# Joining the pair sums of the first two rounds on VectorE in 45 more attention jobs, and a later start for the last unit's W1 loads

## The chip, the core and the metric

The kernel is one program on one core of a Trainium2 chip. The metric is the device time of one execution in microseconds (us). The core has five engines with a queue each: TensorE (PE) multiplies matrices into the accumulator memory PSUM, ScalarE (ACT) evaluates functions, VectorE (DVE) adds, multiplies and copies, GpSimd (POOL) does small helper work, and SyncE (SP) starts all transfers. Each engine takes its instructions strictly in the order in which they were written, and waits at an instruction until the semaphores that it names have their values.

## The reference: a transformer layer

The input x has 2048 tokens of 1024 values, in bf16.

```python
h  = x + softmax((Q @ K.T) * 32**-0.5) @ V  joined over 32 heads of 32, @ wo    # Q, K, V = layernorm(x) @ wqkv
h2 = h + gelu_tanh(layernorm(h) @ w1 + b1) @ w2 + b2                             # w1: 1024 x 3584, w2: 3584 x 1024
```

Softmax needs, for each head and query, the sum of its 2048 exponentials. The kernel leaves out the maximum, keeps exp(scores) unnormalised in bf16, multiplies it with V, and divides by that sum at the end.

## The kernel before

**Jobs and rounds.** Queries are cut into 8 blocks of 256 (`qb` 0 to 7), heads into 8 groups of four (`g`). One pair (qb, g) is a job of 8 rounds; a round treats 256 keys. In a round PE computes the scores of four heads with 8 matmuls (`Att.qk`, line 838) into four PSUM banks; ACT turns them into probabilities with two exponentials of 128x1024 (line 850) written to a tile PT of a ring of nine. Then PE multiplies them with V (`Job.pv`, line 879). There are 512 rounds, or 1024 exponentials. The score step of a round needs PSUM banks that an earlier exponential has emptied. Groups 6 and 7 of the blocks 6 and 7 are done as two halves of 128 queries and 4 rounds each, so that the last unit can be finished half by half.

**The sums.** The denominators come from PE too: a matmul with a matrix of ones (`den`, line 918) adds up the probabilities over the keys of a tile. To spare PE, VectorE first adds the two 128-key halves of a round's tile PT into a tile PS (line 894, 128x1024 in bf16); `den` then takes 4 matmuls for a round instead of 8. The last round of a job is summed directly from PT. In whole jobs of the query blocks 6 and 7 (`four`, with the rounds in `FOURS`) the PS tiles of rounds 0 and 1, 2 and 3, 4 and 5 are also added to each other (line 901, the join), so that one `den` serves two rounds. PS is a ring of three tiles. When the job is over, five small VectorE instructions (lines 936 to 949) divide and write the attention output OT.

**The three lead jobs** (g = 0, qb = 0 to 2) run while the projections are still being computed; they sum every second round directly.

**Feed-forward work.** It is cut into 8 units of 256 tokens. For unit u, `wo` projects the attention output and adds x, `ln2` normalises, `ffn1` multiplies with W1 in 14 blocks of 512 KB (tile a_w1r, a ring of four), `evict1` (line 1049) adds the bias, `gelu` does five VectorE steps and a tanh on ACT (line 1067), and `ffn2` multiplies with W2 in two column halves j of 7 blocks each (tile a_w2r, a ring of seven). This work needs the attention of its own query block and fills PE between the rounds of later blocks. Unit 7 is done by halves of 128 tokens at the end: `wo(7)`, `ln2(7)`, `ffn1_half` and `ffn2_tile`; its W1 blocks are loaded once, to 14 places of their own (`W1B`, tile w1b), where K and V of the head groups 0 to 6 have been, and the second half of W2 goes to the tile w2b, where PT has been.

**The matmul helper.** `mm` writes a matmul either as one instruction (line 599 or 602) or as four of 32 columns (line 596) when it stands among other column-tiled ones.

**The order.** No engine's order is written out by hand. Every operation is a `Task` with engine, cost, priority and the tasks that it depends on, and `Graph.schedule` plays the program through once at build time with a table of costs and writes down the order that comes out. For PE it takes a ready score step first, then probabilities times V and sums, then feed-forward matmuls. On VectorE a lower number goes first: -2 for the sums and joins, 0 for evictions, 1 for gelu. On SP large loads of priority 1 may have three and of priority 2 two before them under way. A change of a dependency therefore moves instructions everywhere after it, on all engines, and the order is then fixed.

**Loads of the last unit's W1.** `load_w1_last` makes the 14 loads with priority 2; each waits for the last reader of the K or V that it overwrites. Between the profile's 899 and 1025 us they are issued among those of a_w1r, wov and a_w2r.

The tail of the program is this:

```python
    ffn1(6)
    load_w1_last()
    wo(7, (0,))
    ffn2(6, 0)
    ln2(7, (0,))
    ffn2(6, 1)
    ffn1_half(0, False)
    wo(7, (1,), True)
    ln2(7, (1,), True)
```

Of the kernel before, what the change touches and what calls it, by code (L numbers as in the profile page):

```python
# [12 lines left out]
P = 128  # L13
# [345 lines left out]
def build_kernel(nc, A_x, A_wqkv, A_wo, B_w1, B_b1, B_w2, B_b2, out):  # L359
# [7 lines left out]
    DC = D // P  # L367
# [9 lines left out]
    gr = Graph(N_LANES)  # L377
# [77 lines left out]
    for kind, k in (("x", 1), ("W", 4), ("x", 0), ("x", 2), ("x", 3), ("W", 3), ("W", 5), ("W", 0), ("W", 1)):  # L455
        h, b = sb(ph0, ("xnT%d" if kind == "x" else "Wall%d") % k, [P, DC, 512], BF, 1, 4)
# [19 lines left out]
    for k in range(2):  # L476
        h, b = sb(xq_lo, "xq%d" % k, [P, DC, 512], BF)
# [87 lines left out]
    def slot(nrel=1):  # L565
        return Slot(gr.buf(), nrel, (6, 7))
# [48 lines left out]
    def dma(out_ap, in_ap, nbytes, reads=(), writes=(), prio=0, noncontig=False, after=()):  # L615
        def fn(s):
            if noncontig:
                with nc.allow_non_contiguous_dma(reason="strided gather"):
                    return s.dma_start(out_ap, in_ap)
            return s.dma_start(out_ap, in_ap)  # L620
        return gr.add(E.SP, fn, 0.06, 0.0, reads, writes, prio, nbytes=nbytes, after=after)
# [234 lines left out]
    PV_START = 7  # L856

    closing = set()
    FOURS = (0, 2, 4)

    class Job:

# [8 lines left out]
        def pv(self, r, s):  # L871
            g, bank, first, nq = self.g, self.bank, self.n == 0, self.nq
            kt = 512 // nq
            last = self.n == self.nr - 1
            self.n += 1
            fns = []
            for i in range(kt):
                for h in range(4):
                    fns.append(lambda p, i=i, h=h: p.matmul(  # L879
                        psum[32 * h:32 * h + 32, bi(bank), 0:nq], V[:, g, kt * r + i, 32 * h:32 * h + 32],  # L880
                        PTs[s][:, h // 2, h % 2, nq * i:nq * i + nq], start=first and i == 0, stop=last and i == kt - 1,
                        tile_position=(0, 32 * h), skip_group_check=True))
            rd = B_PTs[s] + B_V[NT * g + kt * r:NT * g + kt * r + kt]
            t = pe(fns, 0.2222 if kt == 2 else 0.2255, reads=rd, writes=[self.B_O, self.B_D] if first else [self.B_O], kind="pv", mode="col")
            take(t, bank)
            while self.sums:
                self.den(*self.sums.pop(0), False)
            if last or self.g == 0 and self.qb < NLJ and r % 2:
                self.sums.append((s, True))
            else:  # L890
                n = cnt["ps"] % NS
                cnt["ps"] += 1
                pairs = PTs[s][:, :, :, :].rearrange("p u j c -> p (u j) c")
                dve(lambda v: v.tensor_tensor(PS[:, n, :, :], pairs[:, :, 0:256], pairs[:, :, 256:512], ALU.add), c_dve(1024, 2),  # L894
                    reads=B_PTs[s], writes=[B_PS[n]], prio=-2, after=hold if self.g == 0 and self.qb < NLJ else ())
                four = nq == 256 and self.qb >= 6
                if four and r in FOURS:
                    self.half = n
                elif four and r - 1 in FOURS:
                    o = self.half  # L900
                    dve(lambda v: v.tensor_tensor(PS[:, n, :, :], PS[:, n, :, :], PS[:, o, :, :], ALU.add), c_dve(1024, 2),
                        reads=[B_PS[n], B_PS[o]], writes=[B_PS[n]], prio=-2)
                    self.sums.append((n, False))
                else:
                    self.sums.append((n, False))
            if last:
                while self.sums:
                    self.den(*self.sums.pop(0), not self.sums)
                self.finish()
# [70 lines left out]
    def wblock(R, src_ap, prio=1, block=None):  # L980
        s = R.next("w1", R.nw1)
        if block is not None:
            dma(R.w1[:, s, :, :], w1d[block], P * DC * 512, reads=[B_w1d[block]], writes=[R.B_w1[s]], prio=prio)
            return s
        dma(R.w1[:, s, :, :], src_ap.rearrange("(dc p) c -> p dc c", p=P), P * DC * 512, writes=[R.B_w1[s]], prio=prio)
        return s
# [48 lines left out]
    def ffn1(u):  # L1035
        R = R1
        for blk in range(FC // 2):
            s = wblock(R, None, block=blk)
            bank = slot()
            for f in range(2):  # L1040
                for dc in range(DC):
                    mm(bank, R.w1[:, s, dc, f * P:(f + 1) * P], hnT[:, dc, :], dc == 0, dc == DC - 1,
                       [R.B_w1[s]] + B_hnT, True, (256 * f, 256 * f + 256))
            evict1(u, gT, B_gT, 2 * blk, 2, 256, bank)
            if blk % 2:
                gelu(gT, B_gT, 4 * (blk // 2), 4, 256)
# [22 lines left out]
        dve(lambda v: v.tensor_tensor(g, w, g, ALU.mult), c_dve(m, 2), reads=b + [B_uu[i]], writes=b, prio=1)  # L1069

    w1_last = []

    def load_w1_last():
        for k, (h, b) in enumerate(W1B):
            dma(h[:, :, :], w1d[k], P * DC * 512, reads=[B_w1d[k]], writes=[b], prio=2)
            w1_last.append((h, b))

    def ffn1_half(t, tail):
# [69 lines left out]
    NLJ = 3  # L1148
# [282 lines left out]
```

## Time and profile before

| what | value |
|---|---|
| runs | 1072.92, 1080.01, 1078.2 us; median 1078.2 |
| profiled execution | 1075.04 us, span of its instructions 1073.2 |
| granted TensorE clock | 1.00 |
| busy: PE, ACT, DVE, POOL | 1043.1, 1008.1, 783.6, 49.1 us |
| exponentials into PT (line 850) | 992, busy 924.6 us |
| pair sums PS from PT (line 894) | 427, busy 280.2 us, mean 685 ns |
| joins (line 901) | 36, median 691 ns |
| matmuls with ones (line 918) | 1692 from PS, busy 108.7 us |
| 512 KB loads, median to landing | a_w1r 4.2, a_w2r 4.6, w1b 3.9 us |

The profile is one execution. "Busy" is the time in which an engine had at least one instruction under way; on PE the ends of matmuls are modelled, so that a full PE is not a PE at its peak. Instructions that follow each other overlap at their ends, so the distance from start to start is shorter than the mean duration. The idle time of an engine that does not set the end costs nothing.

### The profile page before, as it was taken

What the parts mean: (1) busy time and instruction counts of PE and PEld (TensorE: products, weight loads), DVE (VectorE), ACT (ScalarE), POOL (GpSimd) and SP (SyncE); (2) the same over time, 40 slices, a digit from 0 to 9 for tenths busy, and PEclk for the clock granted to TensorE, in tenths of its full rate; (3) what the DMA queues carried; (4) which work ended last, traced back from release to release, by engine and by line L of the source; (5) the groups of instructions that cost most, each with busy time, mean ns of one, the idle gap of its engine ahead of it and who ended that gap; (6) DMA issues with size and microseconds to landing.
All of it is one profiled execution on the core that took longest, in us unless ns stands there. A gap on an engine that the chain in (4) does not pass through costs nothing.

```text
span 1073.2 us, 39708 instructions
## 1 busy us (share of the span) xinstructions
PE 1043.1 (97%) x17978; PEld 605.2 (56%) x17978; DVE 783.6 (73%) x1521; ACT 1008.1 (94%) x1117; POOL 49.1 (5%) x110
## 2 busy tenths in 40 slices
PE   8999999999999999999999999999999999998998
PEld 6576555554445744664475466447546644663575
DVE  8766666566677995797499569759978958987560
ACT  4999999999999999999999999999999999999732
POOL 4200000000000010001000000100010000000000
PEclk9999999999999999999999999999999999999999
DMA  8460544334665546846565684656377444876530
GB/s 236 110 184 23 175 135 120 120 119 153 207 207 160 193 160 187 281 148 217 185 222 173 179 271 166 220 177 227 125 237 253 173 153 148 271 265 227 202 131 16
DMA packets 130649, 192.04 MB, mean 179 GB/s; under 512 B 47024, under 2 KB 95024, under 8 KB 127920
## 3 DMA queue, kind: packets, MB, share of 16 engines
q1 hardware_dynamic: 130480, 189.50, 54.3%
q8 instruction: 141, 2.31, 0.8%
q14 instruction: 28, 0.23, 0.1%
HBM read 175.32 MB, written 26.21 MB: 188 GB/s over the span
## 4 chain that ended last, share of the span: by engine, by line
PE 61%; ACT 31%; DMA 3%; DVE 3%; issue 1%; POOL 0%; SPq 0%; DVEq 0%; POOLq 0%
PE ps L599 29%; ACT PT L850 28%; PE ps L838 10%; PE ps L596 7%; PE ps L879 7%; PE ps L918 4%; PE ps L602 3%; ACT PX L850 2%; DMA a_w2r<-w_blocks 2%; ACT uu L1067 2%; DMA a_w1r<-w_blocks 1%; DVE PS L894 1%; PE ps L1144 1%; PE ps L669 0%; DVE hch L1121 0%
## 5 line engine op out<-in xcount | busy, mean ns | idle before, releaser
L850 ACT ACTIVATE PT<-ps 128x1024 bf16<-128x1024 f32 x992 | 924.6, 1176 | 9.1 <-PE ps L838 8.6
L894 DVE TENSOR_TENSOR PS<-PT 128x1024 bf16<-128x1024 bf16 x427 | 280.2, 685 | 76.9 <-PE ps L918 39.0
L838 PE MATMUL ps<-QT,KT 32*128 32x256 bf16 (+1 forms) x4352 | 203.6, 266 | 9.3 <-ACT PT L850 6.6
L879 PE MATMUL ps<-PT,V 128*32 128x256 bf16 (+1 forms) x4224 | 160.6, 267 | 3.0 <-ACT PT L850 1.8
L838 PEld LDWEIGHTS ps<-QT,KT 32*128 32x128 bf16 x4352 | 64.4, 92 | 163.9 <-ACT PT L850 149.4
L599 PE MATMUL ps<-a_w2r,gT 128*128 128x512 bf16 x609 | 152.1, 381 | 4.5 <-DVE gT L1069 1.6
L599 PE MATMUL ps<-hnT,a_w1r 128*128 128x256 bf16 x1165 | 143.3, 273 | 2.7 <-DMA a_w1r<-w_blocks 2.2
L599 PEld LDWEIGHTS ps<-hnT,a_w1r 128*128 128x128 bf16 x1165 | 107.0, 98 | 33.6 <-issue 17.8
L879 PEld LDWEIGHTS ps<-PT,V 128*32 128x32 bf16 x4224 | 101.5, 97 | 25.7 <-issue 8.9
L918 PE MATMUL ps<-PS,ones 128*32 128x256 bf16 (+1 forms) x1692 | 108.7, 268 | 1.0 <-DVE PS L894 0.8
L599 PEld LDWEIGHTS ps<-a_w2r,gT 128*128 128x128 bf16 x609 | 52.0, 98 | 74.7 <-issue 19.7
L1049 DVE TENSOR_TENSOR gT<-ps,b1f 128x512 bf16<-128x512 f32 x98 | 67.4, 687 | 21.2 <-PE ps L596 13.1
L599 PE MATMUL ps<-xnT,Wall 128*128 128x512 bf16 (+1 forms) x364 | 79.9, 355 | 0.2 <-ACT xnT L676 0.2
L1067 ACT ACTIVATE uu<-uu 128x1024 bf16<-128x1024 bf16 (+1 forms) x53 | 61.6, 1182 | 14.2 <-DVE uu L1066 14.2
L1121 DVE SCALAR_TENSOR_TENSOR hch<-ps,hch 128x512 bf16<-128x512 f32 x32 | 21.9, 685 | 72.5 <-PE ps L599 39.3
L596 PE MATMUL ps<-hnT,a_w1r 128*32 128x256 bf16 x1612 | 61.0, 274 | 2.1 <-issue 1.7
L599 PE MATMUL ps<-wov,OT 128*128 128x512 bf16 x224 | 56.0, 380 | 0.0
L918 PEld LDWEIGHTS ps<-PS,ones 128*32 128x32 bf16 x1692 | 43.0, 96 | 18.9 <-DVE PS L894 6.7
L653 POOL CAST mvb<-mv 128x2 bf16<-128x2 f32 (+1 forms) x25 | 6.3, 253 | 983.0 <-DVE mv L650 983.0
L596 PE MATMUL ps<-a_w2r,gT 128*32 128x512 bf16 x700 | 50.2, 381 | 0.0
L599 PEld LDWEIGHTS ps<-xnT,Wall 128*128 128x128 bf16 x364 | 31.2, 98 | 32.8 <-issue 9.6
L596 PEld LDWEIGHTS ps<-hnT,a_w1r 128*32 128x32 bf16 x1612 | 40.8, 96 | 12.4 <-issue 10.7
(102 smaller groups left out, 995.6 us busy)
## 6 DMA issues: line engine op xcount, KB each, us to landing
a_w2r<-w_blocks SPq DMA_DIRECT2D x105, 512.0 KB, 4.6
a_w1r<-w_blocks SPq DMA_DIRECT2D x98, 512.0 KB, 4.2
wov<-wo_blocks SPq DMA_DIRECT2D x16, 1024.0 KB, 4.8
w_blocks<-in_B_w_dram SPq DMA_DIRECT2D x28, 512.0 KB, 3.9
w1b<-w_blocks SPq DMA_DIRECT2D x14, 512.0 KB, 3.9
Wall<-in_A_wqkv_dram SPq DMA_DIRECT2D x17, 256.0 KB, 4.5
xrb<-in_A_x_dram SPq DMA_DIRECT2D x16, 256.0 KB, 5.0
a_w1r<-in_A_wqkv_dram SPq DMA_DIRECT2D x8, 512.0 KB, 4.8
```

The source lines that it names most:

```text
L596: fns.append(lambda p, j=j: p.matmul(psum[32 * j:32 * j + 32, bi(bank), c0:c1], lhsT[:, 32 * j:32 * j + 32], rhs, start=start, stop=stop, ...
L599: t.whole = lambda p: p.matmul(psum[:, bi(bank), c0:c1], lhsT, rhs, start=start, stop=stop, skip_group_check=True)
L602: t = pe(lambda p: p.matmul(psum[:, bi(bank), c0:c1], lhsT, rhs, start=start, stop=stop), occ, reads=reads, writes=[bb(bank)], mode="full" ...
L838: return p.matmul(psum[:, 2 * us[h // 2] + h % 2, n * i:n * i + n], KT[32 * h:32 * h + 32, g, k0:k0 + P], QT[32 * h:32 * h + 32, qs, q0:q0 ...
L850: act(lambda a, u=u, k=k: a.activation(PTs[s][:, k, :, :], psum[:, 2 * u:2 * u + 2, :], ACT.Exp, bias=0.0, scale=SCALE), 1024, reads=[B_ps ...
L879: fns.append(lambda p, i=i, h=h: p.matmul(psum[32 * h:32 * h + 32, bi(bank), 0:nq], V[:, g, kt * r + i, 32 * h:32 * h + 32], PTs[s][:, h / ...
L894: dve(lambda v: v.tensor_tensor(PS[:, n, :, :], pairs[:, :, 0:256], pairs[:, :, 256:512], ALU.add), c_dve(1024, 2), reads=B_PTs[s], writes ...
L918: fns.append(lambda p, h=h, rhs=rhs, i=i: p.matmul(psum[32 * h:32 * h + 32, bi(bank), 256:256 + nq], ones32[:, :], rhs, start=False, stop= ...
L1049: t = dve(lambda v: v.tensor_tensor(g[:, fc:fc + nf, :], psum[:, bi(bank), :].rearrange("p (f c) -> p f c", f=nf), b1f[:, fc:fc + nf].unsq ...
L1067: act(lambda a: a.activation(w, w, ACT.Tanh, bias=0.0, scale=KT2), m, reads=[B_uu[i]], writes=[B_uu[i]], prio=-1)
L1121: drop(dve(lambda v: v.scalar_tensor_tensor(hch[:, hs, c], psum[:, bi(bank), :], half, hch[:, hs, c], ALU.mult, ALU.add), c_dve_ps(512), r ...
L1144: pe(lambda p: p.matmul(psum[:, 6, 0:256], ident[:, :], b2t[:, 0:256], start=True, stop=True), 0.18 if k < 42 else 0.115, reads=[B_ident, ...
```

## The change

There are two parts. In the first, the join of rounds 0 and 1 is done in all whole jobs but the three lead jobs; blocks 6 and 7 keep their three joins. In the second, `ffn1(6)` notes its 14 W1 loads, and all 14 loads of the last unit's W1 depend on the eleventh of them (`w1_loads[10:11]`).

```diff
@@ Job.pv
-    FOURS = (0, 2, 4)
...
-                four = nq == 256 and self.qb >= 6
+                four = nq == 256 and not (self.g == 0 and self.qb < NLJ)
+                FOURS = (0, 2, 4) if self.qb >= 6 else (0,)
                 if four and r in FOURS:
                     self.half = n
                 elif four and r - 1 in FOURS:
@@ ffn1
             s = wblock(R, None, block=blk)
+            if u == 6:
+                w1_loads.append(gr.tasks[-1])
@@ load_w1_last
+    w1_loads = []
...
-            dma(h[:, :, :], w1d[k], P * DC * 512, reads=[B_w1d[k]], writes=[b], prio=2)
+            dma(h[:, :, :], w1d[k], P * DC * 512, reads=[B_w1d[k]], writes=[b], prio=2, after=w1_loads[10:11])
```

The join itself is the same code as before:

```python
                    o = self.half
                    dve(lambda v: v.tensor_tensor(PS[:, n, :, :], PS[:, n, :, :], PS[:, o, :, :], ALU.add), c_dve(1024, 2),
                        reads=[B_PS[n], B_PS[o]], writes=[B_PS[n]], prio=-2)
                    self.sums.append((n, False))
```

## The prediction

> **What bounds the kernel now.** I read the totals first, then the 40 slices, then busy time by stage, then ScalarE's waits, the chain, and last the timeline of the end. TensorE (PE) and ScalarE (ACT) look equally full in the totals:
>
> ```profile
> PE 1043.1 (97%) x17978; PEld 605.2 (56%) x17978; DVE 783.6 (73%) x1521; ACT 1008.1 (94%) x1117; POOL 49.1 (5%) x110
> ...
> ACT  4999999999999999999999999999999999999732
> ```
>
> The slices show where ACT is not full: in the first and in the last three. The stages (us, then busy time and count of PE, PEld, VectorE (DVE), ACT, POOL, then clock, DMA share, GB/s) say it in numbers:
>
> ```profile
> 81.30:340.00 258.70, 256.34 (x4370) 135.32 (x4363) 168.07 (x311) 258.63 (x283) 3.99 (x8) 1.00 0.46 141
> 340.00:400.00 60.00, 60.00 (x1089) 38.10 (x1087) 55.24 (x107) 60.00 (x67) 1.53 (x4) 1.00 0.49 175
> ...
> 855.00:920.00 65.00, 59.23 (x1232) 29.43 (x1233) 48.23 (x103) 63.52 (x70) 3.76 (x8) 1.00 0.51 173
> 920.00:962.00 42.00, 39.77 (x767) 28.73 (x769) 37.24 (x68) 40.06 (x45) 0.00 (x0) 1.00 0.76 267
> 962.00:1013.10 51.10, 46.79 (x969) 22.84 (x961) 35.47 (x73) 50.78 (x56) 2.01 (x4) 1.00 0.61 209
> 1013.10:1073.20 60.10, 56.37 (x706) 39.80 (x698) 23.66 (x51) 15.36 (x37) 1.53 (x4) 1.00 0.27 97
> ```
>
> From 81 to 1013 us ACT works without a break: its idle time, stage by stage, sums to 5.8 us of 932. What it does there is fixed: exponentials (one per 0.92 us back to back: 47.79 us for 52 in the chain) and the 49 tanh of units 0 to 6. After 1013.1 it is almost done, and PE carries the last 60.1 us (56.4 busy). So the end is the last exponential plus a PE tail, and time can only come from ACT's 5.8 us or from the tail. ACT's waits in that stretch:
>
> ```profile
> ACT PT L850 <- PE ps L838: 5.6, 9, 1.4
> ACT PT L850 <- PE ps L879: 0.3, 1, 0.3
> ```
>
> Always a late score matmul. The larger ones are 1.08 us at 423 (PE waited 1.40 for W2), 1.25 at 881 (PE's 1.16 before it is put down to issue), 1.36 at 944 and 0.57 at 961. The last two belong to the second last unit's W1, which the chain shows as loads:
>
> ```profile
> 930.99 5.84 DMA a_w1r<-w_blocks
> ...
> 937.28 5.20 DMA a_w1r<-w_blocks
> ...
> 952.65 4.88 DMA a_w1r<-w_blocks
> ```
>
> These take 4.9 to 5.8 us where the kernel's median for such a load is 4.2, with 267 GB/s moved, since w1b loads for the last unit run between them.
>
> **The joins: what goes, what comes.** Query blocks 0 to 5 have 48 jobs; three lead jobs are left out, so 45 get one join. Each drops one denominator step of 4 column-tiled matmuls, 0.11 us on PE (929.50 in the chain): 45 x 0.11 = **5.0 us of PE**. Each adds one 128x1024 add on VectorE. The rows give it two prices: 0.69 alone (the 36 joins of blocks 6 and 7: median 691 ns) and 2.51 us for four in a row at 739.89, a step of (2.51 - 0.69)/3 = 0.61. Busy engines queue, so I take 0.61: 45 x 0.61 = **27 us of VectorE**, 3% of the 932 us.
>
> The 5.0 us are worth what ACT waits less, not 5.0 us. In the changed program's order the feed-forward work does run ahead: ffn2 of unit 6 ends in score round 506 instead of 512 (a round is one score step and two exponentials, 1.84 us). But wo of unit 7 needs the first half's attention output and begins in round 509, where it began in 507. PE will stand idle instead. Gain between 0 and the 1.6 us of ACT's idle time that neither a load nor issue explains (5.8 less 1.08, 1.25, 1.36 and 0.57 is 1.6); I take **0**, since nothing shows that these fragments come from lack of PE time.
>
> The 27 us of VectorE hide while VectorE has room. At 81 to 340 it is 65% busy. At 340 to 400, a ffn1 stretch, it is 92% busy, and its order is fixed: evictions, gelu steps and sums queue behind each join, and a sum that is late holds PE's next instruction, thus the score matmul. Adding 0.61 per 14.7 us job is +4%, so 96%. The new order spreads it: in unit 2, 42 exponentials (was 33) and 7 tanh stand between the first and last tanh, with 92 VectorE instructions (was 76) for them: 92/49 = 1.88 per ACT step, was 76/40 = 1.90. No denser, but for longer. Bounds: 0 (the stretch 340 to 400 lost nothing at 92%) to 1 us per unit, where a lag of 4% over a stretch of 33 us (18 rounds), 1.3 us, meets the 0.42 us that PE usually waits before a score step in the timeline: 0.9, seven times 6 us. I take **+0.5 us** in all, near the lower end: the 36 joins of today, three per job, ran from 763 to 985 us (at 920 to 962 VectorE was 89% busy), and PE's waits for a joined tile add up to 1.4 us, two in all.
>
> [...]
>
> **The W1 wait.** The 14 w1b loads now wait for load 11 of ffn1(6). On SP's queue the first w1b load stands behind load 12, and loads 13 and 14 stand behind that w1b load. Load 11 issues when its slot is freed in round 475 and lands about 5 us later, near round 478; load 13's slot is free in 477, so it issues one round late, and is used in 482, 4 rounds or 7.3 us on, against 4.2 to 5.8 for a landing. It is covered by 1.5 us; uncovered it would cost what it takes away. Loads 1 to 10 no longer share the engines with w1b. I take away both waits: **-1.9 us**; bounds -1.9 and +1 (a W1 wait elsewhere, the other seen being 0.69).
>
> Behind it, w1b00 to w1b31, wov and W2 move to about 980 instead of 900 to 966: 14 w1b loads of 0.5 MB, 7 MB at 267 GB/s 28 us, and the last exponential is 33 rounds away. The last two w1b loads now stand behind all seven w2b loads; these go out as probability tiles come free, the last about 1 us after the last exponential, so w1b61 lands by +10 us and is wanted at +17. Today it is issued at 1024.69, 11.6 us after the last exponential, and wanted at about +17 too. No price.
>
> **The tail.** Today the last exponential ends at 1013.07, the first w1b matmul starts 4.16 later (1017.23), and the span ends 55.97 after that. In the new order 17 of the last tile's 18 output-projection matmuls stand before the first w1b matmul (8 today), one behind. Step by step after the last exponential: final sum and PV 0.85; its normalisation 1.75, beside seven projection matmuls; then five at 0.215, 1.1; transposes 0.45; copy to hnT 0.7; latencies 0.3. That is 5.1, so +0.9. Nine matmuls fewer behind: -9 x 0.215 = -1.9. Sum **-1.0**; bounds -2 (today's 0.69 gap at 1020 goes too) and +1 (gelu gates the interleaved W2 matmuls).
>
> **Sum:** 0 + 0.5 - 1.9 - 1.0 = -2.4 us. The profiled execution took 1075.04 (span 1073.2 and 1.8 around it): 1072.6. The median of the runs, 1078.2, lies 3.2 above; from it, 1075.8. I predict between them, **1074**.
>
> **Rivals.**
> *The waits only move.* W1's 1.9 us come back at W2 (the 423 us kind, 1.08) or as a late wov: a 1 MB load lands in 4.5 to 6.6 us, and the new order, counted in rounds of 1.84, leaves 5.2 us from freed slot to use in four places; today's least is 4.9, without a stall. Then -0.5: 1075 to 1077. For: DMA is already 0.76 busy. Against: same bytes.
> *VectorE becomes the bound* (slower). Place: the seven ffn1 stretches. Price: 0.9 us each is +6.3, less the 2.9 gained elsewhere: 1078; at twice that, if each late eviction also holds a PSUM bank, 12.6 - 2.9: 1085. It decides once a stretch's lag exceeds the 0.42 us and (2.9/7) 0.4 more. For: 92 to 95% busy there. Against: instruction density is unchanged, and ACT lost nothing at 340 to 400.
> *ACT never waits again.* All 5.8 us and 2 of the tail: -7.8, so 1067 by the profiled time and 1070 by the median. For: PE has 5 us in hand. Against: the issue wait and W2's are not PE work.
> *The sums go elsewhere*, so the change does nothing: excluded, the changed program has 180 ones-matmuls fewer and 45 adds more.
>
> **Numbers.** Forecast (-5 to 0) 0.55, moved waits 0.17, VectorE 0.17, no ACT wait 0.11. The range reaches into the last two, and runs of one kernel differ by 7 us (1072.9 to 1080.0): **1065 to 1083**. One per cent, 10.8 us, is about what a measurement of this kernel can tell from no change; -10.8 needs more than everything ACT and the tail can give unless runs scatter (half of that rival's 0.11 and a tenth of the forecast: 0.11); +10.8 needs the VectorE rival at or above its upper price (0.10); within, 0.79.
>
> **What the changed profile would show.** Right: ones-matmuls down by 180; ACT idle from 81 us to the last exponential 3 to 5 us; no a_w1r load in the chain near 930 to 960 and those loads near 4.2 us; first w1b matmul about 5 us after the last exponential; VectorE near 95% in ffn1 stretches with PE's waits for its tiles under 15 us. Wrong: PE waiting for summed or evicted tiles for over 0.5 us inside ffn1 stretches with score matmuls late behind it; w1b or W2 loads ending the chain after 960; ACT idle above 8 us.

## The result, and the profile after

| | before | after |
|---|---|---|
| median of 22 runs, side by side | 1076.13 us | 1080.99 us |
| ratio after / before | | 1.0039, 95% interval 1.0025 to 1.0054 |
| profiled execution, span | 1075.04, 1073.2 us | 1077.76, 1075.8 us |
| last exponential ends | 1013.1 us | 1017.7 us |
| from there to the end of the span | 60.2 us | 58.2 us |
| ACT idle from 81 us to the last exponential | 6.0 us | 11.1 us |
| first matmul with w1b after the last exponential | 4.2 us | 4.7 us |

The change makes the kernel slower, by 0.4%, some 4 us; the forecast was a small gain. In the profiled pair the tail gets 2.0 us shorter, as hoped, but the last exponential comes 4.6 us later, because ACT waits 5.1 us more.

The totals and two rows of the 40 slices of after. ACT has an 8 in slice 33 where it had a 9, and a 2 in slice 39 where it had a 3; the granted clock (PEclk) has an 8 in slice 35:

```profile
PE 1043.9 (97%) x17579; PEld 601.9 (56%) x17579; DVE 815.6 (76%) x1566; ACT 1008.1 (94%) x1117; POOL 49.6 (5%) x110
...
ACT  4999999999999999999999999999999989999722
...
PEclk9999999999999999999999999999999999899999
```

The work itself changed as planned. The groups of after (busy us, mean ns, then idle time before them): the ones-matmuls from PS went from 1692 to 1512, the joins from 36 to 81, at 0.69 us each. The last two numbers of the exponentials are the loss: 14.4 us of waits instead of 9.1, all but a little for score matmuls. None of it is a direct wait of ACT for VectorE:

```profile
L850 ACT ACTIVATE PT<-ps 128x1024 bf16<-128x1024 f32 x992 | 924.3, 1185 | 14.4 <-PE ps L838 14.0
...
L918 PE MATMUL ps<-PS,ones 128*32 128x256 bf16 (+1 forms) x1512 | 97.0, 268 | 1.2 <-issue 0.6
...
L901 DVE TENSOR_TENSOR PS<-PS 128x1024 bf16<-128x1024 bf16 x81 | 55.5, 685 | 1.5
```

The stretches of after say where (us; then busy time and count of PE, PEld, DVE, ACT, POOL, then clock, DMA share, GB/s):

```profile
340.00:400.00 60.00, 59.67 (x1023) 36.53 (x1016) 57.33 (x113) 60.00 (x67) 4.00 (x8) 1.00 0.47 164
...
866.00:870.00 4.00, 4.00 (x223) 3.11 (x224) 2.40 (x4) 4.00 (x6) 0.00 (x0) 1.00 0.87 263
870.00:873.00 3.00, 0.29 (x16) 0.16 (x16) 1.46 (x5) 0.80 (x1) 0.00 (x0) 1.00 0.22 81
873.00:878.00 5.00, 5.00 (x74) 2.00 (x73) 2.15 (x8) 3.86 (x4) 0.00 (x0) 0.66 0.01 3
...
908.00:915.00 7.00, 4.11 (x96) 1.57 (x84) 6.48 (x13) 7.00 (x9) 1.31 (x3) 0.99 0.78 282
915.00:922.00 7.00, 6.79 (x69) 3.54 (x69) 5.12 (x12) 6.05 (x7) 1.44 (x2) 0.52 0.01 4
...
962.00:1017.70 55.70, 49.17 (x1075) 24.30 (x1067) 35.50 (x73) 52.17 (x57) 0.00 (x0) 1.00 0.76 265
1017.70:1075.80 58.10, 54.99 (x626) 38.61 (x626) 22.62 (x47) 15.47 (x37) 3.27 (x8) 1.00 0.20 66
```

In 340 to 400, VectorE is 95.6% busy and ACT still loses nothing: the crowded ffn1 stretch is not the place. Three other places are. At 870 PE does almost nothing for 3 us, and then works 5 us at a clock of 0.66. At 915 to 922 the clock is 0.52. After 962, ACT is short by 3.5 us.

**The stall at 870.** The timeline of PE in after (start, us, tiles, count):

```profile
866.71 1.32 PE L878 MATMUL ps<-PT,V 128*32 128x128 bf16 x80
867.87 0.28 PE L918 MATMUL ps<-PS,ones 128*32 128x128 bf16 x8
867.98 0.40 PE L878 MATMUL ps<-PT,V 128*32 128x128 bf16 x16
...
869.43 0.40 PE L878 MATMUL ps<-PT,V 128*32 128x128 bf16 x16
869.73 0.29 PE L918 MATMUL ps<-PS,ones 128*32 128x128 bf16 x8
869.96 0.29 PE L838 MATMUL ps<-QT,KT 32*128 32x128 bf16 x8
872.96 0.29 PE L838 MATMUL ps<-QT,KT 32*128 32x128 bf16 x8 [2.71 <-issue]
```

These are half jobs of block 6: 128 queries, so that each matmul has 128 columns and takes some 14 ns from start to start (80 in 1.16 us). 208 of them stand between 866.71 and the stall at 870.25, without a large feed-forward matmul in between. Then PE waits 2.71 us in the middle of a score step, eight matmuls done and eight to go, for nothing that the profile can name ("issue"). In before, the same work came in two bursts with large feed-forward matmuls between them. The second one:

```profile
873.84 1.69 PE L599 MATMUL ps<-a_w2r,gT 128*128 128x512 bf16 x7
...
876.23 0.62 PE L879 MATMUL ps<-PT,V 128*32 128x128 bf16 x32
...
877.58 0.28 PE L879 MATMUL ps<-PT,V 128*32 128x128 bf16 x6
879.01 0.34 PE L879 MATMUL ps<-PT,V 128*32 128x128 bf16 x10 [1.16 <-issue]
```

What it waits for can be read from a queue that moves next to nothing. The DMA queues of after (packets, MB, share of the engines):

```profile
q1 hardware_dynamic: 130480, 189.50, 53.3%
q8 instruction: 138, 2.26, 0.8%
```

Before has 141 such packets, of 16 KB each. PE's weight loads and matmuls together are 35956 in before and 35158 in after: 255 per packet in both. By this count queue 8 carries PE's own program, some 255 of these instructions at a time. The trace's record of single packets gives the rest: the one that belongs to the stall ran from 870.71 to 871.67 us, and PE went on at 872.96, 1.3 us later. Eight stalls of 0.3 us or more end in after between 534 and 1017 us, and each ends 1.2 to 1.6 us after the end of such a packet; in before it is the same for those at 535.8, 632.5, 759.4 (0.24 us), 851.7, 879.0, 998.0 and 1020.2. The last four of after, at 1003.2, 1006.7, 1010.7 and 1017.0 us, are 255, 256 and 256 weight loads and matmuls apart: each falls on the step from one packet to the next. By these times I read the stalls as PE waiting for its instructions; the profile itself names nothing. What delays the packet was not tried; between 866 and 870, DMA is 87% busy.

Behind this stall, and behind the gap at 908 to 915, the clock is at one half. The trace's clock record of after has it at 0.50 from 873.9 us for 3.4 us and from 914.9 us for 6.8 us; before has no such drop ahead of its last 2 us. In the drops a score step takes 0.61 us (875.41 and 916.50), behind them 0.40 (878.02 and 922.17). Ahead of the first drop PE idles 2.71 us, ahead of the second it is busy 4.11 us of 7 (908 to 915). Not every long stall is followed by a drop: in e3 below, PE idles 3.53 us up to 299.8 us, and the score step behind it takes 0.40 us (300.38), as does the one ahead of it (295.57).

### The profile page after: what moved, and what is told of

It reads as the page before. It is cut to its first block, busy times and chain, and to the rows that moved or that the text cites. A ratio compares the mean times of both kernels' runs of the same rounds, so it can differ in the third digit from the quotient of the medians.

```text
span 1075.8 us, 38988 instructions
## 1 busy us (share of the span) xinstructions
PE 1043.9 (97%) x17579; PEld 601.9 (56%) x17579; DVE 815.6 (76%) x1566; ACT 1008.1 (94%) x1117; POOL 49.6 (5%) x110
## 4 chain that ended last, share of the span: by engine, by line
ACT 68%; PE 26%; DVE 3%; issue 1%; DMA 1%; POOL 0%; DVEq 0%
ACT PT L850 63%; PE ps L599 11%; PE ps L838 4%; ACT uu L1069 3%; PE ps L602 3%; PE ps L878 3%; PE ps L596 3%; ACT PX L850 2%; PE ps L918 2%; DVE PS L893 1%; DMA q_scratch<-lq 1%; PE ps L1147 0%; DVE st L648 0%; PE ps L669 0%; DMA xrb<-in_A_x_dram 0%
## 5 line engine op out<-in xcount | busy, mean ns | idle before, releaser
L850 ACT ACTIVATE PT<-ps 128x1024 bf16<-128x1024 f32 x992 | 924.3, 1185 | 14.4 <-PE ps L838 14.0
L893 DVE TENSOR_TENSOR PS<-PT 128x1024 bf16<-128x1024 bf16 x427 | 285.6, 686 | 89.4 <-PE ps L918 45.8
L599 PE MATMUL ps<-hnT,a_w1r 128*128 128x256 bf16 x1242 | 153.0, 274 | 0.2 <-DVE rr L946 0.2
L599 PEld LDWEIGHTS ps<-hnT,a_w1r 128*128 128x128 bf16 x1242 | 114.6, 98 | 33.0 <-issue 19.2
L918 PE MATMUL ps<-PS,ones 128*32 128x256 bf16 (+1 forms) x1512 | 97.0, 268 | 1.2 <-issue 0.6
L599 PE MATMUL ps<-xnT,Wall 128*128 128x512 bf16 (+1 forms) x388 | 85.9, 356 | 0.4 <-ACT xnT L676 0.3
L901 DVE TENSOR_TENSOR PS<-PS 128x1024 bf16<-128x1024 bf16 x81 | 55.5, 685 | 1.5
L596 PE MATMUL ps<-a_w2r,gT 128*32 128x512 bf16 x684 | 52.5, 386 | 2.5 <-issue 2.3
L599 PEld LDWEIGHTS ps<-xnT,Wall 128*128 128x128 bf16 x388 | 33.1, 98 | 35.9 <-issue 11.1
L596 PE MATMUL ps<-hnT,a_w1r 128*32 128x256 bf16 x1304 | 48.9, 274 | 2.2 <-issue 2.2
L918 PEld LDWEIGHTS ps<-PS,ones 128*32 128x32 bf16 x1512 | 38.6, 96 | 17.0 <-issue 6.6
L599 PE MATMUL ps<-wov,OT 128*128 128x512 bf16 x183 | 45.5, 381 | 1.3 <-DVE OD L943 0.8
```

The costliest lines, as they stand in the source:

```text
L596: fns.append(lambda p, j=j: p.matmul(psum[32 * j:32 * j + 32, bi(bank), c0:c1], lhsT[:, 32 * j:32 * j + 32], rhs, start=start, stop=stop, ...
L599: t.whole = lambda p: p.matmul(psum[:, bi(bank), c0:c1], lhsT, rhs, start=start, stop=stop, skip_group_check=True)
L850: act(lambda a, u=u, k=k: a.activation(PTs[s][:, k, :, :], psum[:, 2 * u:2 * u + 2, :], ACT.Exp, bias=0.0, scale=SCALE), 1024, reads=[B_ps ...
L918: fns.append(lambda p, h=h, rhs=rhs, i=i: p.matmul(psum[32 * h:32 * h + 32, bi(bank), 256:256 + nq], ones32[:, :], rhs, start=False, stop= ...
```

## The experiments

Ratios are to runs of the kernel before on the same chip, with 95% intervals. "The order of after" means that every engine has its instructions as in after. In the trace of before, VectorE's 1521 instructions stand, by the tiles that they write, in the order in which they were written.

### The two parts alone

The joins without the W1 wait (e1):

```
-            dma(h[:, :, :], w1d[k], ..., prio=2, after=w1_loads[10:11])
+            dma(h[:, :, :], w1d[k], ..., prio=2)
```

> Part one alone: the 45 joins, with the loads of the last unit's W1 waiting for nothing new. Three theories of the +0.4%. (A) PE is starved: for instructions, and by a granted clock that falls where the feed-forward work runs out. The trace of after shows 9.1 us of stalls that end 1.2 to 1.6 us after a 16 KB instruction transfer (before: 4.1 us) and a clock of 0.50 to 0.57 near 916 to 922. The first comes from chance and from what transfers run beside it, the second from the joins (work that runs ahead leaves a gap). Then joins alone cost +1 to +4 us against before, with a clock below 1.00 in the gap before ffn1(6). (B) The joins' VectorE time costs the loss: +3 to +6 us, and PE waits for VectorE's tiles are longer than in before. (C) The loss is part two's, since its loads now run beside the last exponentials: joins alone are -2 to 0 us.

Measured: **1.0049** (1.0029 to 1.0068), some 5.3 us. That is above the range of theory (A) and inside that of (B), so the next runs have to decide between the two.

The wait without the joins (e2):

```
-                four = nq == 256 and not (self.g == 0 and self.qb < NLJ)
-                FOURS = (0, 2, 4) if self.qb >= 6 else (0,)
+                four = nq == 256 and self.qb >= 6
+                FOURS = (0, 2, 4)
```

> Part two alone: the kernel before, with the 14 loads of the last unit's W1 waiting for the eleventh load of ffn1(6). (A) and (B): a gain of up to the 1.9 us of the two W1 waits, so -2 to 0 us against before, with PE's instruction stalls between 960 and 1020 us at the 1.1 us of before or little more. (C) its loads, now beside the last exponentials, delay instruction transfers and W2: +2 to +4 us, with stalls of 3 us or more between 960 and 1020.

Measured: **1.0010** (0.9991 to 1.0028), no change. Its profile shows why the 1.9 us do not arrive: the W1 waits at 944 and 961 are gone (ACT idle 0.0 us between 935 and 985), and one instruction stall after them is larger than any of before:

```profile
998.15 0.29 PE L838 MATMUL ps<-QT,KT 32*128 32x128 bf16 x3 [2.25 <-issue]
```

So the loss is part one's. Theory (C) falls. The stall that (C) expected did come, but it only takes back the gain.

### Is it the joins, the freed time, or the order?

The joins have three effects: VectorE does 45 more adds, PE does 180 matmuls less, and the planner, seeing both, writes another order. They were taken apart. First, the order of after with 45 joins of 8 columns, which leave VectorE busy for 795.2 us instead of 815.6 (e3):

```
-  PS[:, n, :, :], PS[:, n, :, :], PS[:, o, :, :]
+  PS[:, n, :, 0:m], PS[:, n, :, 0:m], PS[:, o, :, 0:m]      # m = 8 for qb < 6, else 256
```

> The order of after on every engine, but the 45 new joins add 8 of 256 columns only, so that their VectorE time is gone (about 27 us less busy) and no instruction moves. The denominators of these jobs leave out almost all of round 0. (A) and (C): VectorE's time is not the price, so the same as after within 1 us (+3 to +5 us against before). (B): the loss goes with it, -1 to +1 us against before.

Measured: **1.0021** (1.0000 to 1.0042), some 2.3 us, between the ranges of the two theories.

Then the order of after with PE's time given back (e4):

```
+            if not direct and n == self.twice:
+                fns = fns + fns
```

> The order of after on every engine, but the 45 joined sums are given to PE twice, 8 matmuls with ones instead of 4: PE's 5.0 us and its instructions are back, VectorE's joins stay. The denominators of these jobs count rounds 0 and 1 twice. If the freed PE time is worth nothing (the prediction's term of 0), the same as after within 1 us. If it is worth its own length, +5 us against after, +8 to +9 us against before. If (A) holds through the freed time opening the gap, at or below after: the same order with fuller PE has a clock nearer to 1.00 at 914 to 922, and the time is 0 to 3 us shorter than after.

Measured: **1.0040** (1.0017 to 1.0063), as after. Then both edits at once (e6):

> The order of after, with the work of before put back: the 45 joins add 8 of 256 columns, and PE does their matmuls with ones twice. The denominators of these jobs are wrong in round 0. (A, order) the loss stays though neither the joins nor the freed time are there: +3 to +5 us against before. (B, VectorE) 0 to +1 us.

Measured: **1.0051** (1.0030 to 1.0073). Of the change's work only the 45 short joins are left in it (in f2 below, VectorE is busy for 788.3 us with them, in before for 783.6), and the order of after is as slow as after. This is the main result: the loss stays when the work goes, so it lies in the order.

The other way round, the work in the order of before. The joins are planned at no cost, and round 0's matmuls stay in the plan but are cut short (e5):

```
+   dve(lambda v: v.tensor_tensor(PS[:, n, :, :], PS[:, n, :, :], PS[:, o, :, :], ALU.add), 0.0, ...)
...
+            if self.cut and not direct and n == self.first:
+                m, self.cut = 8, False
```

> The order of before on every engine (12 PE instructions of 17980 stand elsewhere), with the work of part one put into it: the 45 joins are done, and round 0's four matmuls with ones are cut from 256 columns to 8, which frees nearly the same PE time. No W1 wait. The denominators of these jobs count 8 columns of round 0 twice. (A, order) The loss is not in the work but in where the feed-forward work comes to stand: without the move the same as before or better, -2 to +1 us against before, with the clock at 1.00 near 916 and no stall of over 2 us near 877. (B, VectorE) The joins themselves cost: +3 to +5 us against before. (C) freed PE time is a gain that the new order hides: -3 to -5 us.

Measured: **1.0021** (1.0004 to 1.0039). Only the joins, with round 0's matmuls whole (f1):

> The order of before, unchanged but for 12 of PE's instructions, with the 45 joins added on VectorE and nothing taken from PE: round 0's matmuls with ones stay whole. The denominators of these jobs count round 0 twice. It measures the price of the joins by itself. (B, VectorE) +2 to +5 us against before; the prediction's term was +0.5, its upper bound +6. (A, order) -1 to +1.5 us.

Measured: **1.0028** (1.0006 to 1.0050). Only the freed PE time, with joins of 8 columns (f2):

> The same order, with PE's time freed and no joins: round 0's four matmuls with ones are cut to 8 columns in the 45 jobs, and the joins add 8 of 256 columns. The denominators of these jobs leave out round 0. It measures what freed PE time is worth where it stands. The prediction's term was 0, its bounds 0 to -1.6 us. (A) -1.6 to +0.5 us against before; more than -3 would say that PE's own work was the bound.

Measured: **1.0022** (0.9999 to 1.0045). Three kernels that do different things, all at +0.2 to 0.3%: so the base that they share had to be measured too, with neither joins nor freed time (h1):

> The common base of the three kernels in nearly the order of before: 45 joins of 8 of 256 columns, all matmuls with ones whole; neither the joins' VectorE time nor the freed PE time is in it. The denominators count a sliver of round 0 twice. If it is 0.2 to 0.3% slower than before, as the three were (1.0021, 1.0028, 1.0022), then the 12 PE instructions and the one W2 load that stand elsewhere make that difference, and the joins and the freed PE time are worth 0 within 2 us each. If it is at 1.000, the joins cost 3 us (the prediction took 0.5, VectorE's theory 3 to 6) and so does freeing PE, which no theory has.

Measured: **1.0019** (1.0000 to 1.0038). So about all that the three lose is in their base. It differs from before by 12 PE instructions, one W2 load, a few VectorE steps and one tanh that stand elsewhere, and by the 45 short joins; no run separates these. Without this base f1 would have spoken for the VectorE theory (+3.0 us, in its +2 to +5), and e5 and f2 against theory (A).

The eight kernels (after, e3 to e6, f1, f2 and h1) give four differences of their ratios for each effect, in us:

| effect | the four differences | mean |
|---|---|---|
| the joins' full length | f1 - h1 +1.0, e5 - f2 -0.1, after - e3 +1.9, e4 - e6 -1.2 | +0.4 |
| the freed PE time | f2 - h1 +0.3, e5 - f1 -0.8, after - e4 -0.1, e3 - e6 -3.2 | -1.0 |
| the order, with nearly the same work | after - e5 +1.9, e4 - f1 +1.3, e3 - f2 -0.1, e6 - h1 +3.4 | +1.6 |

Each difference is uncertain by some 3 us, a mean of four by some 1.5. Neither a price of the joins nor a gain from the freed time shows; one of 2 us isn't excluded. The order of after is clearly slower than before (e6), but only 1.6 us of that, hardly clear of the noise, lie between it and kernels nearly in the order of before. The other 2.4 us are what these lie above before.

### Where the order loses it

One profile is one execution, and its waits vary. But seven profiles share the order of after or nearly so (after, e1, e3, e4, e6, and below e7 and g1), and five that of before (before, e5, f1, f2 and h1). Mean idle time of ACT, up to the last exponential, and the tail behind it, in us:

| stretch (us) | what waits there | before | after | five, mean | seven, mean | difference |
|---|---|---|---|---|---|---|
| 290 to 330 | PE for lq or wov | 0.0 | 0.2 | 0.5 | 2.2 | +1.7 |
| 840 to 895 | PE for instructions, then the slow clock | 1.5 | 3.8 | 2.2 | 4.2 | +2.0 |
| 895 to 935 | the slow clock behind a gap | 0.0 | 1.6 | 0.2 | 1.3 | +1.1 |
| 935 to 985 | PE for W1 (in after: for instructions) | 2.0 | 1.1 | 2.5 | 0.3 | -2.2 |
| 985 to the last exponential | PE for instructions | 0.3 | 2.4 | 0.4 | 4.9 | +4.5 |
| all others from 81 | | 2.3 | 2.0 | 2.8 | 3.2 | +0.4 |
| the tail | | 60.2 | 58.2 | 61.7 | 58.2 | -3.5 |

The sum of the last column is +4.0 us. The gains that were meant are in it, -2.2 for W1 and -3.5 in the tail, 5.7 us together; the four stretches that grow lose 9.3 (+1.7, +2.0, +1.1, +4.5). These are means of single executions, some of them the slowest of their kernel (e1, e7, e5); by all runs the ratios of the same kernels differ by 0.22% in the mean, 2.4 us. Clear of the scatter is the stretch behind 985 us, 2.4 to 7.5 us in the seven and 0.2 to 0.7 in the five. At 840 to 895 it is 3.4 to 5.5 against 1.5 to 3.6. The +0.4 of "all others" comes from e7 alone, whose prologue differs (see below).

The large stall at 870 to 881 us is in all seven profiles, each time on the step from one packet to the next by the count of weight loads and matmuls, with gaps of 2.5 to 3.6 us between two weight loads. It is no accident of one execution.

In the table's first row PE waits for VectorE's copy lq, a part of the late Q projections, which itself waits for an earlier store of lq; so it is in e1, below. In e6, e7 and g1 it waits for a late wov as well, as in the last line, from e6. In the five, e5 and h1 wait for lq too (1.6 and 0.9 us of ACT's time):

```profile
298.12 1.29 DVE L758 CAST lq<-ps 128x512 bf16<-128x512 f32 x2 [4.30 <-DMA q_scratch<-lq]
298.87 0.62 PE L878 MATMUL ps<-PT,V 128*32 128x256 bf16 x16 [2.80 <-DVE lq L758]
...
306.20 0.39 PE L599 MATMUL ps<-wov,OT 128*128 128x512 bf16 x1 [1.95 <-DMA wov<-wo_blocks]
```

### The gap and the clock

In before, the last ffn2 of unit 5 runs until round 463, and ffn1(6) begins in round 467. In after it ends in round 455, the output projection of unit 6 in round 460, and ffn1(6) begins in 466, since it needs that projection and the layer norm behind it. In between (908 to 915) PE is busy 4.11 us of 7, and from 914.9 the clock is 0.50 for 6.8 us. Filled with matmuls of zeros (e7):

```
+            n = 4 if t in qk_round else 4 if t in pv_job else 0
+            if n and job is not None and 460 <= q < 466:
+                fns = [lambda p, h=h: p.matmul(psum[32 * h:32 * h + 32, bi(bank), 256:512], zero32[:, :], b2t[:, 0:256],
+                                               start=False, stop=False, tile_position=(0, 32 * h), skip_group_check=True)
+                       for _ in range(n) for h in range(4)]
```

> After, with 16 matmuls of zeros (0.44 us) behind each score step and each probabilities-times-V step of the rounds 460 to 465, where the output projection of unit 6 is over and ffn1(6) may not begin, so that PE does not idle there. Nothing else moves but a few VectorE steps of the prologue. (A, clock) The granted clock falls to 0.50 for 3.4 to 10.2 us behind this gap in every kernel with the order of after, and never in before; filled, it stays at 1.00 between 910 and 926, ACT's 1.6 us of waits there go, and the time is 1 to 3 us below after. (A without the clock) The slow matmuls behind the gap are due to something else: the clock falls all the same, and the time is that of after or up to 1 us longer.

The clock did as expected; this is the gap of e7, some 9 us later than in after (columns as above):

```profile
910.00:917.00 7.00, 6.99 (x150) 3.39 (x146) 5.44 (x11) 7.00 (x9) 0.00 (x0) 1.00 0.87 273
917.00:924.00 7.00, 5.89 (x165) 3.34 (x157) 6.48 (x13) 7.00 (x9) 1.25 (x3) 1.00 0.89 303
924.00:931.00 7.00, 6.91 (x155) 4.72 (x156) 4.91 (x12) 6.25 (x8) 1.50 (x2) 1.00 0.05 17
```

The time did not: **1.0045** (1.0027 to 1.0063). ACT still idles 0.75 us there, beside an instruction stall of 1.04 us at 924; in after it was 1.57. By these two profiles the clock drop costs some 0.8 us of ACT's time in this gap.

But the time of e7 decides nothing on the clock. More than "a few VectorE steps" moved: its trace has another order than after on VectorE and on PE between 20 and 130 us, and ACT idles 3.9 us at 60 to 110 us, where no other kernel here idles more than 0.6. After, then e7 (columns as above):

```profile
60.00:110.00 50.00, 49.70 (x1076) 33.30 (x1072) 36.05 (x69) 49.70 (x56) 0.00 (x0) 1.00 0.28 70
60.00:110.00 50.00, 47.59 (x1031) 30.84 (x1024) 35.29 (x68) 46.08 (x51) 0.00 (x0) 1.00 0.31 70
```

The difference is 3.6 us, 0.34%. Without it, by this estimate, e7 would lie some 3 us below after, as theory (A, clock) had it. No run here has the filled gap and the prologue of after, so the price of the clock stays open. The fastest kernel below (f3) has a mean clock of 0.57 from 914 to 926 us, some 10 us at one half in the same gap, so the price can at least be made up for elsewhere.

### Instructions

If PE starves for instructions in the bursts of the half jobs, fewer of them should help. Block 6 in whole jobs has half as many matmuls there, of 256 columns and 28 ns from start to start (16 in 0.45 us in e8) where those of 128 took some 14. First in after (e8):

```
-        attention(u + 3, range(G) if u < 3 else range(6) if u == 3 else range(6))
-        if u == 3:
-            for half in range(2):
-                attention_half(6, range(6, G), half)
+        attention(u + 3, range(G) if u <= 3 else range(6))
```

> After, with groups 6 and 7 of query block 6 as whole jobs instead of two halves of 128 queries, so that their probabilities-times-V and ones steps take half as many instructions; the order before them stays. (A, instructions) The stall of 2.5 to 3.6 us near 873 to 877 stands behind some 150 such instructions in 3.3 us, at the boundary of a 16 KB instruction transfer; with half as many it is below 1 us, the clock does not fall behind it, and the time is 2 to 4 us below after. (Otherwise) the stall belongs to the place, through the transfers around it: it stays over 2 us, and the time is that of after within 1 us.

Measured: **1.0000** (0.9984 to 1.0016), so 0.4% below after (1.0039). Between 840 and 895 us ACT idles 0.0 us in its profile; in that of after it was 3.8. The burst is now a string of steps of 256 columns with feed-forward matmuls between, and there is no stall in it:

```profile
872.43 0.62 PE L878 MATMUL ps<-PT,V 128*32 128x256 bf16 x16
872.88 0.28 PE L918 MATMUL ps<-PS,ones 128*32 128x256 bf16 x4
872.99 0.61 PE L878 MATMUL ps<-PT,V 128*32 128x256 bf16 x16
...
874.63 0.82 PE L596 MATMUL ps<-a_w2r,gT 128*32 128x512 bf16 x12
```

The same edit to the kernel before (f3):

> The kernel before, with groups 6 and 7 of query block 6 as whole jobs. (A, instructions) before has only 1.2 us of its instruction stalls at that place (1.16 near 879), so the gain is smaller than the 4 us that it is in the order of after: -2 to 0 us against before. (A gain of the plan itself, whatever the stalls) -3 to -5 us, as in after.

Measured: **0.9960** (0.9943 to 0.9977), and once more (h2):

> The kernel before with whole jobs in block 6, once more: 0.994 to 0.998 of before if its first measurement (0.996) stands.

Measured: **0.9963** (0.9949 to 0.9978), median 1073.37 us. This is faster than both kernels. It is also more than the instruction theory gave for the order of before (0 to -2 us); the gain is the same in both orders. In its two profiles ACT idles 1.0 and 0.6 us at 840 to 895 (2.2 in the mean of the five) and 0.0 us at 935 to 985, where W1 was waited for (2.5): part of it is a stall that went, part of it the new order once more.

e8 against f3 is the change once more, with whole jobs in block 6 on both sides: 1.0000 against 0.9960, the same 0.4%. So the stall of the half jobs at 870 us is a loss that both orders can be spared, but the change costs as much without it (0.4% is uncertain by 0.2). In these two profiles ACT idles 3.2 us at 290 to 330 and 2.8 after 985 us in e8, 0.3 and 0.5 in f3.

With the W1 wait added to that (f4):

> The kernel before, with whole jobs in block 6 and with part two (the W1 wait) but not part one. If the two parts stand by themselves, the time of the former plus 0 to -2 us, so -4 to 0 us against before, and this is the version to keep. If part two moves transfers beside the last exponentials and starves PE of instructions there (one stall of 2.3 us at 998 in the profile of part two alone), +1 us against the former.

Measured: **0.9982** (0.9958 to 1.0007). That is 0.2% above f3, nearer to the second expectation than to the first: the wait brings nothing here either. Its profile, one of its two slowest executions, has 6.4 us of ACT's idle time after 985 us.

Fewer instructions without a move, by writing more of the feed-forward matmuls whole, in after (g1) and in f3's kernel (g2):

```
-            if k == 0 or sum(x.occ for x in run[k:]) >= 3.0:
+            if k == 0 or sum(x.occ for x in run[k:]) >= 0.1:
```

> The order of after, unchanged, but every run of feed-forward matmuls that ends a column-tiled run is written as single instructions instead of four of 32 columns (the limit of 3.0 us for it is set to 0.1): some 800 of PE's 17600 matmuls fewer, each four as long as the one that replaces them. (A, instructions) fewer instructions between two 16 KB instruction transfers: the stalls near 873 and after 985 us shrink, -1 to -3 us against after (0 to +0.3% against before). (Otherwise) the same as after within 1 us, or longer, if the change of the tiling costs time at each place.

> The same done to the fastest version so far (before, with whole jobs in block 6, 0.996 of before). (A, instructions) 0 to -2 us against that version, as few stalls are left in it. (Otherwise) +0 to +2 us.

Measured: **1.0036** (1.0016 to 1.0055) and **0.9968** (0.9951 to 0.9984), so nothing in either. The stall near 877 is still there (ACT idles 4.5 us between 840 and 895). The instructions that this removes aren't those of the bursts, which are the attention's own.

The end, with group 6 of block 7 as a whole job, in after (g3) and in f3's kernel (g4):

```
-        attention(u + 3, range(G) if u < 3 else range(6) if u == 3 else range(6))
+        attention(u + 3, range(G) if u < 3 else range(6) if u == 3 else range(7))
...
-    attention_half(7, range(6, G), 0)
-    attention_half(7, range(6, G), 1)
+    attention_half(7, range(7, G), 0)
+    attention_half(7, range(7, G), 1)
```

> After, with group 6 of block 7 as a whole job, so that only group 7 is done by halves at the end. (A, instructions) the six profiles with the order of after wait 2.4 to 7.5 us on ACT after 985 us, behind four half jobs in a row; with two of them gone that is 1 to 3 us, and the time 2 to 4 us below after, unless the tail becomes longer than its 58.2 us. (Otherwise) the waits after 985 us stay.

> The fastest version so far, with group 6 of block 7 as a whole job too. Its profile has only 0.45 us of ACT's waits after 985 us, so there is little to gain: -1 to +2 us against that version, the upper end if the tail (60.5 us) grows.

Measured: **1.0042** (1.0025 to 1.0059) and **1.0009** (0.9994 to 1.0025). In g3's profile ACT idles 0.0 us after 985 us, where the seven idle 4.9 on average: the four half jobs in a row made those waits. But its tail is 61.7 us instead of 58.2 (in g4 65.6 instead of 60.5). The halves are there for the tail, and pay for themselves. The same edit costs 0.3 us in the order of after and 5.3 us in f3's kernel, which had no such waits to lose: this pair says that the waits after 985 us cost the order of after some 5 us, give or take 3.5.

What those waits look like in after, one packet of instructions after the other; the packets that belong to them ended at 1001.68, 1005.26, 1009.32 and 1015.50 us:

```profile
1003.15 0.82 PE L596 MATMUL ps<-a_w2r,gT 128*32 128x512 bf16 x10 [1.22 <-issue]
...
1006.72 0.23 PE L918 MATMUL ps<-PS,ones 128*32 128x128 bf16 x2 [0.56 <-issue]
...
1010.74 0.40 PE L878 MATMUL ps<-PT,V 128*32 128x128 bf16 x14 [0.73 <-issue]
...
1016.95 0.35 PE L878 MATMUL ps<-PT,V 128*32 128x128 bf16 x11 [0.58 <-issue]
```

In before, ffn2(6) lasts until round 512 and its large matmuls stand between the half jobs; in after it is done in round 506.

## Why the prediction was wrong, step by step

**What bounds the kernel: right, but taken as fixed.** The end is the last exponential plus a tail, in both kernels. I listed the 5.8 us of ACT's waits in one profile and asked only which of them would go. I didn't ask which would come. The waits marked "issue" I put down as something that no term had to explain, and that was the second chance missed: the 1.16 us at 879 was the small version of what became 2.71.

**Freed PE time, 0: the step that failed.** As the worth of 5.0 us less PE work, 0 isn't contradicted: in held orders the four differences are +0.3, -0.8, -0.1 and -3.2 us, each uncertain by some 3. But the sentence "PE will stand idle instead" and its price of 0 are where the sum broke. It looked at the rounds in which feed-forward work ends, saw that it runs 2 to 6 rounds ahead, and took running ahead as harmless. What I should have read in the new order is what is left when that work is gone: score, V and ones steps of the half jobs in a row, and a gap before ffn1(6). The missing term is the price of the new order. With nearly all the work taken out again it alone measures +0.5% (e6), and in the profiles it shows as ACT's waits: +4.5 us after 985, +2.0 at the half jobs of block 6, +1.7 for lq and wov, +1.1 in the gap. How the 4 us net divide among these stays open; the first is the best supported (g3 and g4), the second is put in doubt by e8 and f3.

**The joins, +0.5: not contradicted.** The four pairs of kernels with and without their full length in a held order give -1.2 to +1.9 us, +0.4 in the mean, uncertain by some 1.5. VectorE was 95.6% busy in 340 to 400, as forecast at 96%, and ACT lost nothing. The VectorE rival, the only one that had the right sign, had it for a reason that the runs don't bear out, so its sign was luck.

**The W1 wait, -1.9: right at its place, wrong in the sum.** Those waits are nearly gone (-2.2 in the table), and the a_w1r loads land in 3.8 us where 4.2 stood. Two things were not seen. The wait isn't needed for it: with the joins alone ACT idles 0.0 us there too. And alone it changes nothing (1.0010). This is the rival "the waits only move", which I gave 0.17; in e2 the wait moved to an instruction stall, which that rival didn't name. The late wov that it did name came true at 306 us in e6, but 600 us before these loads, so part two didn't bring it. Its price, half a microsecond less gain, fits part two alone (+0.1%) and not the change.

**The tail, -1.0: right in sign, -2.0 in the pair of profiles.** The first w1b matmul comes 4.7 us after the last exponential (5.1 was worked out), and from there to the end of the span it is 53.4 us, 2.6 less than 56.0 (1.9 was worked out).

**What I had named as signs.** Right: 180 ones-matmuls fewer, no a_w1r load late, the first w1b matmul, VectorE at 95% without late tiles in 340 to 400. The sign against it came true as well: ACT idles 11.1 us, above the 8 that I had set.

**Range and chances.** The median, 1081, lies inside 1065 to 1083, near its upper end, and "within 1%" holds; both owe that to the width that I gave them and not to the sum, which had -2.4 us where the runs have some +4. The base of 1078.2, a median of three runs, was itself 2 us above that of 22. Most of the chance stood on a small gain or none, from a sum that had no term for the order.

**A small slip.** The idle time left after the four larger waits is 1.5 us, not 1.6; nothing hangs on it.

## What to carry to other kernels

Where a planner writes the order, price the order and not only the edit: put the plan's new order next to the old one, and look at the stretches from which work has moved away, as closely as at those to which it goes. Here the order lost more than 45 small instructions could bring. And count instructions per microsecond: the 208 matmuls of the burst at 867 us, with as many weight loads, take 3.54 us, so that at 255 to a packet they use up one every 2.2 us, by this estimate, and the stall at the step to the next packet held PE for 2.71 us, without a name in the profile. Holding the order while taking the work out showed that the loss stays. But measure the base of what the holding itself moves, which was half of the loss here, and compare the traces' orders engine by engine before you trust that an order was held: in e7 it was not.

## What the runs showed of the hardware that I had not expected

- By the count, PE's program arrives in DMA packets of 16 KB: 141 in before and 138 in after, one for each 255 weight loads and matmuls. In both, the stalls that I put down to them end 1.2 to 1.6 us after a packet has landed; a packet takes 0.96 us in the median. In after, a burst that ran through its last 256 weight loads and matmuls in 2.4 us (867.8 to 870.2) waited 2.71.
- In after, the granted clock drops to 0.50 for 3.4 us behind a single stall of 2.71 us, and for 6.8 us behind 7 us with PE 59% busy; behind a stall of 3.53 us in e3 the score step took 0.40 us as before it. The time so given up, (1 - clock) x span, is 6.8 us in the mean of the 22 runs of after and 2.1 in 35 of before; within after's runs it goes with the time (0.93 us for 1, correlation 0.74). Whether it is a cause or a mark of the stalls the runs don't say: e7 has 3.6 us of it and is as slow as after, but with another prologue, and the fastest kernel has 4.7.
- A dozen PE instructions and one load in other places, with 45 joins of 8 columns on VectorE, moved the time by 0.2% (0.00 to 0.38), about as much as the parts of this change that were meant.
